# First tails issued by GpSimd, first copy in halves, roots ahead of tables, warming from a constant: the opening of a fused scan and gated-MLP kernel

## Chip, core, metric

The kernel runs on one core of a Trainium2 chip. A core has TensorE (PE in the profile), VectorE (DVE), ScalarE (ACT), GpSimd (POOL), SyncE (SP) and 16 DMA engines that SP, ACT and GpSimd can issue to. The metric is device time in microseconds (us).

## The reference, cut to what matters

```python
xn = layernorm(x)                        # x: 2048 tokens of 448, bf16
Lam_bar = exp(exp(log_dt) * Lam)         # 448 complex states
h[t] = Lam_bar * h[t-1] + B_bar @ xn[t]  # B_bar: 448 x 448 complex
s = 2 * real(h @ C.T) + xn * Dskip
gate, up = xn @ w_gate, xn @ w_up        # 448 -> 1792 each
g = silu((sigmoid(gate) * up) @ w_down)  # 1792 -> 448
out = x + s * g
```

## The kernel before

The 2048 tokens are four chunks (`c`) of 512, and a chunk is four tiles (`j`) of 128 tokens. Products need xn turned, with the 448 features on partitions and tokens along the row: `xnT[c]`, of four blocks of rows (`kt`). A chunk's products are those of the gate and up weights (`g_ps`, `u_ps`, 14 column blocks `ft`), those of B (`bu`), of the down weights (`d_ps`) and of C (`y_ps`). The contraction over 448 is cut into three full blocks of 128 and a tail of 64 rows. The tails of gate and up share a tile: `wt`, gate on partitions 0 to 63 and up on 64 to 127. A gate tail and an up tail then run beside each other in the two halves of the array; L709 issues those of chunk 0. The eight PSUM banks are handed out in turn, so a product that opens a bank waits for the reader of its former content.

The weights come in three parts of column blocks (`w_parts`): part 1 is `gate_1`, `up_1` and `tails_1` (columns 0 to 511). All loads but one of `gate_1` go through SP, and a load is issued only when the one eight places earlier (counting SP's and ACT's) has landed.

The order on each engine is the written order (`keep_order` ties every instruction to the one before it on its engine). Around the change it is this:

- SP issues the loads of x for chunk 0 (tile 0, tile 1, then 2 and 3 together), then part 1 of the weights, `tails_1` last, then part 2, tiles of x of chunk 1, and the transposing loads of B (`bT`).
- TensorE runs 26 products of a zeroed tile `junk` (`warm`), turns the three vectors of the scan (`tp_v`), runs 5 more, turns tile 0 (four turns into `tps[0]`, L289), 2 more, tile 1, 2 more, and then the first gate products on tiles 0 and 1 (`firsts`, L713). Tile 2 and tile 3 are turned between the up products.
- DVE sets constants, takes the moments of tiles 0 and 1 (`ln_stats`: L219, L220), norms both (`ln_norm`, L275), copies the turned tile 0 out of PSUM (`ln_out`, L292), takes the moments of tiles 2 and 3, norms them and copies both.
- ACT takes the root of the variance of a tile in two steps (`ln_inv`, Ln and Exp: L252, L253), tiles 0 and 1, copies the turned tile 1, makes the first rounded angle table (`emit_whole(0)`, L427), takes the roots of tiles 2 and 3, makes the other three tables, loads the table of sine functions and makes sines and cosines (`tables`). Between them come the tanh of chunk 0's first gates (L719).
- GpSimd makes `ident` and a row of indices, and then waits for `dt_b` of ACT (L324), from which it makes `theta`, `turn` (read by `emit_whole`) and `arg_r` (L329 to L331) and the steps of the scan. Later it also relays semaphores: where a sum passes from one half of the array to the other, a `nop` of GpSimd waits for the one product and releases the next (`Sum.add`).

Of the kernel before, what the change touches and what calls it, by code (L numbers as in the profile page):

```python
# [11 lines left out]
BF16 = mybir.dt.bfloat16  # L12
# [7 lines left out]
P = 128  # L20
# [4 lines left out]
KT = 4  # L25
# [47 lines left out]
def kernel(  # L73
# [17 lines left out]
    nc = tc.nc  # L91
    pe, act, dve, pool, sync = nc.tensor, nc.scalar, nc.vector, nc.gpsimd, nc.sync
# [16 lines left out]
    xnT = [w.tile([P, KT, TC], BF16, name=f"xnT{c}") for c in range(3)]  # L109
# [15 lines left out]
    def w_parts(f0, f1):  # L125
        def rows(mat, r0, r1):
            m = mat[r0:r1, f0:f1]
            return m.rearrange("(kt p) f -> p kt f", p=P) if r1 - r0 > P else m

        gate = [(wg[:, 1:3, f0:f1], rows(B_w_gate, 192, 448)), (wg[:, 0, f0:f1], rows(B_w_gate, 0, 128))]  # L130
        up = [(wu[:, 0:2, f0:f1], rows(B_w_up, 0, 256)), (wu[:, 2, f0:f1], rows(B_w_up, 320, 448))]
        tails = [(wt[0:64, f0:f1], rows(B_w_gate, 128, 192)), (wt[64:128, f0:f1], rows(B_w_up, 256, 320))]
        return gate, up, tails

    def load(eng, parts):
        return [eng.dma_start(out=o, in_=i) for o, i in parts]
# [15 lines left out]
    gate_1, up_1, tails_1 = w_parts(0, 512)  # L152
    gate_2, up_2, tails_2 = w_parts(512, 1280)
# [4 lines left out]
    def load_x(c, j0=0, j1=TPC):  # L158
        if c == 3:
            x_t.append(w.tile([P, TPC, D], BF16, name="x3", tag="tc_re"))  # L160
        sync.dma_start(out=x_t[c][:, j0:j1, :], in_=x_src[:, c * TPC + j0:c * TPC + j1, :])
# [15 lines left out]


    junk = w.tile([P, D], BF16, name="junk")
    dve.memset(junk[:, 0:P], 0.0)  # L180
    hpi = w.tile([P, 1], FP32, name="hpi")
    dve.memset(hpi[:], HALF_PI)
    sgn = w.tile([P, 1], FP32, name="sgn")
# [14 lines left out]

    warm_ps = ps.tile([P, P], FP32, name="warm_ps", tag="bank", bufs=8)

    def warm(n, t=ident):
        for _ in range(n):
            pe.matmul(warm_ps[:], lhsT=t[:, 0:P], rhs=t[:, 0:P], start=True, stop=True)  # L203

    def turn_twice(o, src, n):

        for kt in range(3):
            pe.transpose(o[:, kt, 0:n], src[:, kt * P:(kt + 1) * P], ident[0:n, 0:n])
        pe.transpose(o[:, 3, 0:n], src[:, D - P:D], ident[0:n, 0:n])
        pe.transpose(o[0:64, 3, 0:n], src[:, 384:D], ident[0:n, 0:n])  # L210


    mv = w.tile([P, NT, 2], FP32, name="mv")
# [3 lines left out]
    def ln_stats(t):  # L217
        stats = cp.tile([P, 6], FP32, name="stats")
        dve.bn_stats(out=stats[:], in_=x_t[t // TPC][:, t % TPC, :])  # L219
        dve.bn_aggr(out=mv[:, t, :], in_=stats[:])  # L220


    sums = w.tile([P, NT, 2], FP32, name="sums")
# [27 lines left out]
    def ln_inv(t):  # L251
        act.activation(lnv[:, t, :], mv[:, t, 1:2], ACT.Ln, bias=epsb[:])  # L252
        act.activation(rsd[:, t, :], lnv[:, t, :], ACT.Exp, scale=-0.5)  # L253
# [29 lines left out]
    def ln_turn(c, j):  # L283
        xb, cols = xn[c % 3], slice(j * P, (j + 1) * P)
        if c > 0:
            sync.dma_start_transpose(out=xnT[c][:, 0:KT, cols], in_=xb[:, j, :])
            return
        for kt in range(KT):
            pe.transpose(tps[j % 2][:, kt, :], xb[:, j, K_ROWS[kt]:K_ROWS[kt] + P], ident[:])  # L289

    def ln_out(j, by_act=False):
        (act.copy if by_act else dve.tensor_copy)(out=xnT[0][:, :, j * P:(j + 1) * P], in_=tps[j % 2][:])  # L292
# [29 lines left out]
    def emit_dt():  # L322
        vec, dt_b = K["vec"], w.tile([P, KT], BF16, name="dt_b")
        act.activation(dt_b[:], vec[:, :, 0], ACT.Exp)  # L324
        K.update(dt=dt_b, lim=vec[:, :, 1], lre=vec[:, :, 2])
# [99 lines left out]
    def emit_whole(pt):  # L425
        whole = sp.tile([P, HC], I32, name="whole", tag=("ta", "tb", "tcs", "tb")[pt])
        act.activation(whole[:], iota_f[:], ACT.Copy, scale=K["turn"][:, pt:pt + 1])  # L427
        K[pt] = whole
# [480 lines left out]
    def ln_plan(c):  # L909
        own, t0, n = c - 1, c * TPC, 2 if c == 2 else 0  # L910
        for k in range(n):
            at(0, 11 + k, 0.8, lambda t=t0 + k: ln_stats(t))
        t1, m = t0 + n, TPC - n
        steps = [lambda t=t: ln_sum(t) for t in range(t1, t1 + m)] + [lambda: ln_mean(t1, m)]
        steps += [lambda t=t: ln_square(t) for t in range(t1, t1 + m)]
        for k, f in enumerate(steps):
            at(own - 1, (10, 10, 11, 11, 12)[k] if c == 2 else "out%d" % min(k // 2, 3), 0.0, f)
        if n:
            at(0, 12, 0.17, lambda: ln_var(t0, n))
        then = (0, 13) if c == 2 else (own, 1)  # L920
        at(*then, 0.17, lambda: ln_var(t1, m, True))
        at(*then, 0.17, lambda: ln_minus(c))
        at(own, "down0", 0.0, lambda: (ln_pow(t0, TPC), ln_scale(c)))
        for j in range(TPC):
            at(own, "down0", 0.0, lambda j=j: ln_norm(c, j))
        at(own, "down0", 0.0, lambda: [ln_turn(c, j) for j in range(TPC)])

    dummy = w.tile([P, 1], FP32, name="dummy")
    act.add_instruction(mybir.InstLoadActFuncSet(name=nc.get_next_instruction_name(), act_func_set_id=LN_AND_EXP,
                                                 ins=[], outs=[]))  # L930
    warm(26, junk)
    turn_twice(tp_v, rows, 3)
    tps = [ps.tile([P, KT, P], BF16, name="tp_x", tag="bank", bufs=8) for _ in range(2)]
    gus = [(bank("g_ps"), bank("u_ps")) for _ in range(3)]
    warm(5)

    ln_stats(0)
    ln_inv(0)
    emit_vecs()
    ln_stats(1)  # L940
    ln_inv(1)
    emit_dt()
    load(sync, tails_1 + gate_2 + tails_2 + up_2)
    load_x(1, 0, 2)
    emit_angles()
    ln_norm(0, 0)
    ln_turn(0, 0)
    warm(2)
    ln_norm(0, 1)
    ln_turn(0, 1)  # L950
    warm(2)
    ln_out(0)
    ln_out(1, True)
    emit_whole(0)
    for t in (2, 3):
        ln_stats(t)
    for t in (2, 3):
        ln_inv(t)
    for pt in (1, 3, 2):
        emit_whole(pt)  # L960
    act.activation(K["r"][:], K["arg"][:], ACT.Exp)
    act.add_instruction(mybir.InstLoadActFuncSet(name=nc.get_next_instruction_name(), act_func_set_id=SILU_AND_SIN,
# [235 lines left out]
```

## Time and profile before

| | |
|---|---|
| median of 3 runs | 182.26 us (182.23 to 182.44) |
| profiled execution | 182.46 us |
| its span, first to last instruction | 180.7 us |
| mean granted TensorE clock | 0.999 |
| DMA | 14.27 MB, mean 79 GB/s |

Times in the profile are counted from the first instruction of the span. PE's ends are modelled, so TensorE is read by the starts of its products. The bracket behind an instruction gives the idle time of its engine ahead of it and what ended that. SPq lines are DMA issues, which occupy only the queue.

### The profile page before, as it was taken

Reading aid. Unit: us, or ns where it says so; the run is one execution under the profiler, and the core shown is the slowest. Engines: PE = TensorE matmul, PEld = TensorE weight load, DVE = VectorE, ACT = ScalarE, POOL = GpSimd, SP = SyncE. Lnnn points to the kernel's source line nnn. Section 1 sums busy time; section 2 is a strip of 40 time slices with the busy share of each in tenths; the row PEclk is TensorE's granted clock in tenths of the full one; section 3 lists DMA queues with packets and bytes.
Section 4 is the critical chain, followed back from the end, with each engine's and each line's share of the span. In section 5 each row is a group of like instructions: output and inputs, shape, how many; then the busy total and the mean of one; then the engine's idle time right before and its main releaser. Section 6 shows DMA issues by size and latency. Waiting matters only on the chain.

```text
span 180.7 us, 4400 instructions
## 1 busy us (share of the span) xinstructions
PE 176.2 (98%) x1672; PEld 100.2 (55%) x1672; DVE 164.8 (91%) x333; ACT 114.1 (63%) x237; POOL 20.0 (11%) x52
## 2 busy tenths in 40 slices
PE   7999999999999999999999999999999999999992
PEld 7875555555555555555555555555555555545451
DVE  4879999999979999899999999699999989599993
ACT  4799988978099887979177676057048577053100
POOL 3504549321000000001000000000000000000000
PEclk9999999999999999999999999999999999999999
DMA  5998993993335105021610020020001100020011
GB/s 156 305 230 156 281 186 63 307 277 91 72 87 106 33 0 131 5 99 29 75 22 4 0 58 4 0 102 4 0 0 34 29 0 5 0 75 32 0 44 58
DMA packets 26364, 14.27 MB, mean 79 GB/s; under 512 B 16099, under 2 KB 26086, under 8 KB 26342
## 3 DMA queue, kind: packets, MB, share of 16 engines
q1 hardware_dynamic: 26064, 13.72, 31.7%
q8 instruction: 13, 0.21, 0.5%
q10 hardware_dynamic: 278, 0.26, 0.4%
q14 instruction: 9, 0.07, 0.2%
HBM read 7.69 MB, written 1.84 MB: 53 GB/s over the span
## 4 chain that ended last, share of the span: by engine, by line
PE 89%; DVE 9%; issue 1%; DVEq 0%
PE g_ps L517 24%; PE u_ps L517 19%; PE d_ps L517 18%; PE bu L517 12%; PE y_ps L517 10%; PE warm_ps L203 2%; DVE wv L614 1%; DVE o_t L831 1%; PE tp_x L289 1%; DVE hF L749 1%; DVE h L635 1%; DVE o_t L833 1%; DVE t_x L848 1%; PE g_ps L713 1%; PE u_ps L713 1%
## 5 line engine op out<-in xcount | busy, mean ns | idle before, releaser
L517 PE MATMUL u_ps<-xnT,wu 64*128 64x512 bf16 (+1 forms) x336 | 64.3, 370 | 0.0
L517 PE MATMUL g_ps<-xnT,wg 64*128 64x512 bf16 (+1 forms) x336 | 57.3, 370 | 0.0
L752 ACT ACTIVATE sig<-g_ps 128x512 bf16<-128x512 f32 x52 | 29.4, 604 | 27.4 <-PE g_ps L517 26.8
L517 PE MATMUL bu<-xnT,bT 64*128 64x512 bf16 x168 | 37.4, 376 | 0.0
L517 PEld LDWEIGHTS <-wu 64*128 64x128 bf16 x336 | 25.8, 94 | 16.6 <-issue 0.3
L517 PE MATMUL d_ps<-wd,hF 64*128 64x448 bf16 x336 | 32.3, 349 | 0.0
L517 PEld LDWEIGHTS <-wg 64*128 64x128 bf16 x336 | 23.1, 94 | 15.9
L752 ACT CAST ub<-u_ps 128x512 bf16<-128x512 f32 x52 | 29.5, 614 | 0.2
L517 PEld LDWEIGHTS <-hF 64*128 64x128 bf16 x336 | 19.0, 94 | 12.9
L614 DVE TENSOR_TENSOR_SCAN wv<-r_col,st,ta 128x512 bf16<-128x512 f32 x18 | 22.7, 1276 | 0.2
L517 PE MATMUL y_ps<-ct,h 64*128 64x448 bf16 (+2 forms) x203 | 22.3, 343 | 0.1
L749 DVE TENSOR_TENSOR hF<-sig,ub 128x512 bf16<-128x512 bf16 x52 | 21.3, 421 | 0.9 <-ACT ub L752 0.8
L517 PEld LDWEIGHTS <-bT 64*128 64x128 bf16 x168 | 15.8, 94 | 8.4 <-issue 0.2
L517 PE MATMUL g_ps<-xnT,wt 64*128 64x512 bf16 x52 | 19.6, 376 | 0.0
L517 PE MATMUL u_ps<-xnT,wt 64*128 64x512 bf16 x52 | 19.6, 376 | 0.0
L517 PEld LDWEIGHTS <-h 64*128 64x128 bf16 (+1 forms) x203 | 12.8, 95 | 8.9 <-DVE h L635 0.5
L595 ACT CAST bus<-bu 128x512 bf16<-128x512 f32 x24 | 14.5, 606 | 1.3 <-PE bu L517 1.3
L776 ACT ACTIVATE sigd<-d_ps 128x448 bf16<-128x448 f32 x12 | 6.7, 555 | 12.3 <-PE d_ps L517 12.3
L517 PEld LDWEIGHTS <-wt 64*128 64x128 bf16 x104 | 9.8, 94 | 5.3
L1141 PE MATMUL d_ps<-wd,hF 128*128 128x448 bf16 x56 | 10.9, 353 | 0.0
L247 POOL TENSOR_TENSOR rsd<-ve,mhalf 128x2 f32<-128x2 f32 (+1 forms) x4 | 4.9, 1213 | 47.9 <-PE bu L517 39.3
L831 DVE TENSOR_TENSOR o_t<-y_ps,xn 128x448 bf16<-128x448 f32 x12 | 6.9, 617 | 3.5 <-PE y_ps L517 3.5
(152 smaller groups left out, 230.5 us busy)
## 6 DMA issues: line engine op xcount, KB each, us to landing
wd<-in_B_w_down_dram SPq DMA_DIRECT2D x1, 1568.0 KB
out_dram<-o_t SPq DMA_DIRECT2D x6, 224.0 KB, 2.1
x<-in_A_x_dram SPq DMA_DIRECT2D x2, 448.0 KB, 4.2
x<-in_A_x_dram SPq DMA_DIRECT2D x3, 224.0 KB, 3.4
wu<-in_B_w_up_dram SPq DMA_DIRECT2D x2, 256.0 KB
bsw<-bus SPq DMA_DIRECT2D x4, 128.0 KB, 4.5
wsw<-wv SPq DMA_DIRECT2D x8, 64.0 KB, 2.0
c_re<-in_A_C_re_dram SPq DMA_DIRECT2D x1, 392.0 KB, 10.0
```

The lines of the kernel that those rows point to most:

```text
L203: pe.matmul(warm_ps[:], lhsT=t[:, 0:P], rhs=t[:, 0:P], start=True, stop=True)
L247: pool.tensor_tensor(out=rsd[:, t:t + n, :], in0=ve[:, t:t + n, :], in1=mhalf[:, 0:n, :], op=ALU.pow)
L289: pe.transpose(tps[j % 2][:, kt, :], xb[:, j, K_ROWS[kt]:K_ROWS[kt] + P], ident[:])
L517: m = pe.matmul(self.t[:, n0:n1], lhsT=lhsT, rhs=rhs, start=self.done == 1, stop=self.done == self.n)
L595: empty = [lambda cc=cc: act.copy(out=bus[:, cc, :], in_=pst[cc][:]) for cc in range(2)]
L614: dve.tensor_tensor_scan(out=T["wv"][:, cc, :], data0=rb, data1=T["ta"][:, cc, :], initial=(0.0 if c == 0 else st[pt][:, cc, :]), op0=mul, ...
L713: pe.matmul(t[:, n0:n1], lhsT=(wg, wu)[i][:, k, ft * P:(ft + 1) * P], rhs=xnT[c][:, (GATE_K, UP_K)[i][k], n0:n1], start=first, stop=last)
L749: dve.tensor_tensor(out=h[:], in0=sig[:], in1=ub[:], op=ALU.mult)
L752: u.empty = [lambda: act.activation(sig[:], gt[:], ACT.Sigmoid), lambda: act.copy(out=ub[:], in_=ut[:])]
L776: act.activation(sigd[:], ds[j][:], ACT.Sigmoid)
L831: dve.tensor_tensor(out=two_runs(o[:, i, :], HD, HD), in0=two_runs(ys[c, j + 2 * i][:], HD, HD), in1=xn_runs(c, j + 2 * i), op=ALU.add)
L1141: pe.matmul(ds[j][:], lhsT=hF[c, ft][:, j * P:(j + 1) * P], rhs=wd[:, ft, :], start=ft == 0, stop=ft == FT - 1)
```

## The change

1. The two loads of `tails_1` are issued by GpSimd in place of SP, behind a semaphore of the first tile's moments. On GpSimd they stand ahead of `theta`.
2. Tile 0's copy out of PSUM is cut in two: ACT copies blocks 2 and 3, DVE blocks 0 and 1. The turns of tiles 0 to 3 are issued in the order 2, 3, 0, 1.
3. `emit_whole(0)` moves from ahead of the roots of tiles 2 and 3 to behind them.
4. The warming products read a constant of ones that the program sets anyway (one column, read 128 times over) in place of `junk`; DVE's memset of `junk` goes, and the first run of warming products is 28 in place of 26.

```diff
     junk = w.tile([P, D], BF16, name="junk")
-    dve.memset(junk[:, 0:P], 0.0)
...
+    ones = nc.const_aps.tensor(1.0, [P, P], BF16)
...
     def ln_stats(t):
         stats = cp.tile([P, 6], FP32, name="stats")
         dve.bn_stats(out=stats[:], in_=x_t[t // TPC][:, t % TPC, :])
-        dve.bn_aggr(out=mv[:, t, :], in_=stats[:])
+        return dve.bn_aggr(out=mv[:, t, :], in_=stats[:])
...
-        for kt in range(KT):
+        for kt in (2, 3, 0, 1):
             pe.transpose(tps[j % 2][:, kt, :], xb[:, j, K_ROWS[kt]:K_ROWS[kt] + P], ident[:])
...
-    warm(26, junk)
+    warm(28, ones)
...
-    ln_stats(0)
+    moments = ln_stats(0)
+    for tail in load(pool, tails_1):
+        tc.add_manual_dep(tail.ins, moments.ins.name,
+                          mybir.DependencyInfo(mybir.DependencyClass.Sync, mybir.DependencyReason.DATA),
+                          reason="behind the first tiles of x")
     ln_inv(0)
...
-    load(sync, tails_1 + gate_2 + tails_2 + up_2)
+    load(sync, gate_2 + tails_2 + up_2)
...
-    ln_out(0)
+    act.copy(out=xnT[0][:, 2:4, 0:P], in_=tps[0][:, 2:4, :])
+    dve.tensor_copy(out=xnT[0][:, 0:2, 0:P], in_=tps[0][:, 0:2, :])
     ln_out(1, True)
-    emit_whole(0)
     for t in (2, 3):
         ln_stats(t)
     for t in (2, 3):
         ln_inv(t)
-    for pt in (1, 3, 2):
+    for pt in (0, 1, 3, 2):
         emit_whole(pt)
```

## The prediction

> **What bounds the kernel now.** I read the page first, for the engine that is never idle:
>
> ```profile
> PE 176.2 (98%) x1672; PEld 100.2 (55%) x1672; DVE 164.8 (91%) x333; ACT 114.1 (63%) x237; POOL 20.0 (11%) x52
> PE 89%; DVE 9%; issue 1%; DVEq 0%
> ```
>
> The second line is the chain that ended last. TensorE carries it, so what this change does to the time is read from when TensorE gets through the opening. DVE's 9% lie at the end of the span, behind products of TensorE, so they move with it.
>
> Next the timeline of the opening, engine by engine (columns: start, length, instruction, count, and in brackets the idle time before it with what ended it). First how a tile of x is turned and copied:
>
> ```profile
> 0.97 2.96 PE L203 MATMUL warm_ps<-junk 128*128 128x128 bf16 x26 [0.97 <-DVE junk L180]
> 4.70 0.63 PE L289 MATMUL tp_x<-ident,xn 128*128 128x128 bf16 x4
> 5.37 0.43 DVE L292 COPY xnT<-tp_x 128x512 bf16<-128x512 bf16 x1
> 5.40 0.61 PE L289 MATMUL tp_x<-ident,xn 128*128 128x128 bf16 x4
> 5.71 0.62 DVE L219 BATCH_NORM_STATS2 stats<-x 128x6 f32<-128x448 bf16 x1
> 6.05 0.58 ACT L292 COPY xnT<-tp_x 128x512 bf16<-128x512 bf16 x1 [1.03 <-PE tp_x L289]
> 7.49 0.82 DVE L275 TENSOR_SCALAR xn<-x,mv,rsd 128x448 bf16<-128x448 bf16 x2 [0.22 <-ACT rsd L253]
> 7.95 0.40 PE L289 MATMUL tp_x<-ident,xn 128*128 128x128 bf16 x4
> 8.38 0.98 DVE L292 COPY xnT<-tp_x 128x512 bf16<-128x512 bf16 x2
> 8.83 0.28 PE L709 MATMUL g_ps<-xnT,wt 64*128 64x256 bf16 x1
> ```
>
> Three things: tile 1's copy on ACT starts 0.65 behind its first turn (5.40 to 6.05). DVE's copy of tile 0 (5.37) stands directly ahead of the moments of tiles 2 and 3 (5.71), and from those come their norms, turns and copies (7.49, 7.95, 8.38). And four turns keep TensorE 0.43 at 4.70 (the next product starts at 5.13) but 0.23 at 7.95: before about 6.3 it runs at half its later rate.
>
> Then ACT and TensorE up to 20.2, for what is tight behind the opening:
>
> ```profile
> 7.78 1.29 ACT L427 ACTIVATE whole<-iota_f,turn 128x256 int32<-128x256 f32 x3
> 12.30 0.60 ACT L719 ACTIVATE tanh<-g_ps 128x512 f32<-128x512 f32 x1 [0.38 <-PE g_ps L517]
> 16.42 0.30 ACT L353 ACTIVATE cs<-anf,hpi 128x8 f32<-128x8 f32 x1 [0.23 <-DVE anf L347]
> ...
> 19.01 1.08 ACT L752 CAST ub<-u_ps 128x512 bf16<-128x512 f32 x2
> ...
> 19.82 0.38 PE L517 MATMUL u_ps<-xnT,wu 64*128 64x512 bf16 x1
> 20.14 0.37 PE L517 MATMUL bu<-xnT,bT 64*128 64x512 bf16 x1
> ```
>
> The second product of bu starts at 20.14 as the second cast of ub ends (20.09): it needs that bank, and TensorE stands about 0.19 (it would have come at 19.96). ACT's work before it runs without a gap back to 16.42, where it waited for DVE; DVE in turn runs nearly without a gap back to a product at 12.27. So a delay of TensorE at 9.8 goes through DVE (12.27), ACT (16.42) and back to TensorE (20.14) at full size. Behind 20.14 TensorE has no gap that could take it up: its one longer wait, 0.27 at 171.1, is for scans that DVE starts after a product at 156.5. What the opening gains or loses reaches the end.
>
> **The change, part by part.** The sum is made against the profiled execution: 182.46 us, a span of 180.7 and 1.76 around it, 0.20 above the median of 182.26. I carry the difference over to the median.
>
> *Warming from a constant.* The first product no longer waits for the memset (0.80 to 0.91). TensorE can start about as early as DVE did, so at 0.85 (between 0.80 and 0.91) instead of 0.97: 0.12 sooner. Two more products cost 2 x 0.107 (2.67 over 25 steps) = 0.21. Net 0.09 later: tile 0's turns start at 4.79. Their norm ended at 4.64, so nothing hides it.
>
> *First copy in halves.* In the changed program the two halves do not run side by side: ACT's half waits for the last of the four turns, and DVE's half waits for ACT's half (they write one tile). So ACT's half starts 0.65 behind the first turn: 4.79 + 0.65 = 5.44. For its length the nearest row is ACT's copy of 128x256 bf16 at L303, 0.44; the other end is 0.37 (the copy of 512 took 0.58, less 256 elements at ACT's slope from the 12-element cast, 0.17). I take 0.44: DVE's half starts at 5.92, where the whole copy started at 5.37. The moments followed the whole copy by 0.34; behind a half I take 0.25 (ends 0.17 and 0.34). So moments of tile 2 at 6.17, 0.46 late (ends 0.3 and 0.55). What waits behind DVE's half: the moments of tiles 2 and 3, then their norms.
>
> *Roots ahead of tables.* One whole (0.41 from start to start) leaves its place ahead of the roots. Tile 2: moments end at 6.55 + 0.46 = 7.01, both root steps take 0.51 (7.36 to 7.87), root at 7.56, not late for a norm that DVE reaches 0.10 behind the start of the last moments, 7.65 (before: 7.49). Tile 3: moments end 7.27 + 0.46 = 7.73, root 8.28 instead of 7.87, norm at 8.32 instead of 7.91. The move hides part of the delay for tile 2, none for tile 3, which waited for its moments and not for the table.
>
> *Turns and copies of tiles 2 and 3.* Tile 2's copy follows the start of tile 3's norm by 0.47: 8.79. Tile 3's follows it by 0.42: 9.21, ends 9.64 (before 9.36). Its products, 9.41 before, start at 9.69: 0.28 late.
>
> *Tails from GpSimd.* They leave SP (0.56 and 0.58 of issue), so all that SP issues later starts up to 1.2 sooner; no row shows TensorE waiting for any of these loads, so that is worth nothing. On GpSimd the two issues wait for the first moments (3.62) and stand ahead of theta (5.10), turn and arg_r (5.89). No row has a DMA from GpSimd. One issue costs between 0.56 (SP's) and 1.1 (GpSimd's longest, the power at L247); I take 0.9: done at 5.5, theta 0.4 late. Now turn is needed only after the roots, at 8.3, and GpSimd first relays a semaphore between two products at 11.1; both have over 1.5 spare, which also is what an issue of over 1.6 each would use up. Landing: the tails took 3.2 (second) from SP and are needed at 8.83, now about 9.1. GpSimd's second issue starts at 4.6: landing at 7.8 with 3.2, at 9.1 with the 4.5 that the next tails took. I count nothing and keep the upper end as a rival.
> Beside these issues DVE runs the norms of tiles 0 and 1 (4.27, 4.95). The same operation shows what a busy GpSimd does to it:
>
> ```profile
> 21.26 1.12 DVE L275 TENSOR_SCALAR xn<-x,mv,rsd 128x512 bf16<-128x512 bf16 x2
> 27.24 0.73 DVE L275 TENSOR_SCALAR xn<-x,mv,rsd 128x512 bf16<-128x512 bf16 x2
> ```
>
> At 21.26 GpSimd copied cosT and spm; at 27.24 it did 128x4 steps. That is 0.2 a norm. Tile 0's norm would end at 4.84 instead of 4.64: its turns at 4.89, 0.10 behind the 4.79 above. I count 0.10 (ends 0 and 0.4).
> [...]
>
> *ACT behind the roots.* Root of tile 3 0.41 + 0.10 late, then four wholes instead of three: tables and sines 0.94 late, tanh(1) at about 12.77, 0.47 behind 12.30. The 0.23 that ACT waited at 16.42, and DVE's own 0.38, cover it with 0.14 spare. Without that cover it would be added.
>
> Sum: 0.28 + 0.10 = 0.38, rounded to 0.39: **182.65**. Ends: 0.05 (short halves, no disturbance) and 0.8 (long halves, norms held 0.4).
>
> **The rivals.**
> *Not slower: the opening loses its two waits.* TensorE stands 0.11 for tile 2's norm (7.84 to 7.95) and 0.08 for tile 3's copy (9.33 to 9.41). If the halves cost DVE less than the whole copy did (its half starting by 5.45), roots come earlier and both go: 182.07; with the 0.19 at 20.14 gone too, 181.88. It decides at ACT's half ending before 5.45, that is, starting near 5.0. For it: turns at the later rate (0.23 for four) would end so. Against: the rate is the slow one in this stage of the trace. Chance 0.14 of a gain over 0.2%.
> *Norms held by GpSimd.* [...] Chance 0.2.
> *Tails late.* From landing after 9.1 on, each microsecond counts whole. With 1.1 an issue and 4.5 to land: 3.62 + 2.2 + 4.5 = 10.3, 1.2 late: 183.85; half of that 183.25. Against: they leave a queue with a backlog for an empty one. Chance 0.10.
> [...]
> *The change is not felt.* The delay ends up at 0.05 to 0.3, since lags shrink where the rate doubles sooner: 182.3 to 182.55. Chance 0.28, and the first rival's milder end lies in it.
>
> **How the numbers follow.** 0.2% of 182.26 is 0.36 us, about what a measurement of this kernel can tell from no change. My forecast (chance 0.28) stands just outside it, the held norms (0.20) and the late tails (0.10) beyond: slower 0.58; a change not felt is same, 0.28; faster 0.14. The likeliest case's own range is 182.3 to 183.0. For 8 in 10 the range goes to 182.0 below (both waits gone) and 183.4 above (tails half late).
>
> **What would show it.** Right: ACT's half copy at 5.4 to 5.5, DVE's half right behind its end, moments of tile 2 at 6.1 to 6.3, tile 3's norm at 8.3, its tail products near 9.7, bu's second product near 20.5. Wrong: DVE's half by 5.5, turns of tile 2 at 7.85 (the first rival); the products of wt waiting for a DMA (tails); norm of tile 0 beyond 4.9 with a gap ahead of it (GpSimd); a table wait of ACT for turn, or a change of the time outside the span.

## The result and the profile after

The changed kernel takes 183.50 us (median of 5, 183.29 to 183.99), the kernel before 182.34 beside it. The ratio is 1.0066, 95% interval 1.0054 to 1.0079: slower by 1.2 us. The profiled execution took 183.44 with a span of 181.7, 0.98 and 1.0 above those of before.

First TensorE's line and the chain that ended last, from the page of the changed kernel:

```profile
PE 176.7 (97%) x1674; PEld 102.7 (57%) x1674; DVE 164.4 (91%) x332; ACT 114.6 (63%) x238; POOL 21.6 (12%) x54
PE 84%; DVE 9%; DMA 4%; issue 1%; POOL 0%; DVEq 0%
```

A share of DMA, 4%, has come into a chain that held TensorE, DVE and some issue. The timeline of the opening shows where (start, length, instruction, count, and in brackets the idle time before it and what ended that). TensorE:

```profile
0.76 3.15 PE L204 MATMUL warm_ps<-const-bfloat16-1.0 128*128 128x128 bf16 x28 [0.76 <-PEq L1187]
4.68 0.63 PE L290 MATMUL tp_x<-ident,xn 128*128 128x128 bf16 x4
7.86 0.40 PE L290 MATMUL tp_x<-ident,xn 128*128 128x128 bf16 x4
8.58 0.40 PE L290 MATMUL tp_x<-ident,xn 128*128 128x128 bf16 x4
9.62 0.28 PE L710 MATMUL g_ps<-xnT,wt 64*128 64x256 bf16 x1 [0.65 <-DMA wt<-in_B_w_gate_dram]
10.09 0.28 PE L710 MATMUL u_ps<-xnT,wt 64*128 64x256 bf16 x1 [0.18 <-DMA wt<-in_B_w_up_dram]
```

Up to tile 3's turns (8.58, before 8.51) TensorE is 0.07 late. Then it stands for the gate tail and again for the up tail, which in the kernel before were both used at 8.83. The first products behind the tails come 1.1 later, in the kernel before and in the changed one:

```profile
9.79 0.27 PE L517 MATMUL g_ps<-xnT,wg 64*128 64x256 bf16 x1
```

```profile
10.87 0.27 PE L518 MATMUL g_ps<-xnT,wg 64*128 64x256 bf16 x1
```

bu's second product starts at 21.23 in place of 20.14, and the last run of y's products at 177.54 in place of 176.45. The delay of 1.1 at 10 us reaches the end. The clock is no part of it: TensorE's full rate starts at 6.3 in both profiles (four turns take 0.61 at 5.40 and 5.42, and 0.40 at 7.95 and 7.86).

DVE and ACT in the same stretch:

```profile
4.24 0.36 DVE L276 TENSOR_SCALAR xn<-x,mv,rsd 128x448 bf16<-128x448 bf16 x1
5.35 0.37 ACT L957 COPY xnT<-tp_x 128x256 bf16<-128x256 bf16 x1 [0.37 <-PE tp_x L290]
5.75 0.29 DVE L958 COPY xnT<-tp_x 128x256 bf16<-128x256 bf16 x1 [0.40 <-ACT xnT L957]
5.96 0.62 DVE L220 BATCH_NORM_STATS2 stats<-x 128x6 f32<-128x448 bf16 x1
8.12 0.40 DVE L276 TENSOR_SCALAR xn<-x,mv,rsd 128x448 bf16<-128x448 bf16 x1 [0.32 <-ACT rsd L254]
9.01 0.42 DVE L293 COPY xnT<-tp_x 128x512 bf16<-128x512 bf16 x1 [0.16 <-PE tp_x L290]
12.48 0.60 ACT L720 ACTIVATE tanh<-g_ps 128x512 f32<-128x512 f32 x1 [0.58 <-PE g_ps L518]
```

The two halves run one behind the other: DVE's waits 0.40 for ACT's. The moments of tile 2 start 0.25 later than before (5.96 for 5.71), and tile 3's copy ends at 9.43 for 9.36. At 12.48 ACT waits 0.58 for TensorE, so in this trace the roots and tables ahead of it cost nothing.

Last the issues that stand behind the wait, GpSimd's and SP's (SPq lines are issues), and from the DMA part of the page what the tails took from issue to landing (KB each, us):

```profile
3.91 0.81 POOL L136 DMA_DIRECT2D wt<-in_B_w_gate_dram  x1 [1.85 <-DVE mv L221]
4.73 0.53 POOL L136 DMA_DIRECT2D wt<-in_B_w_up_dram  x1
```

```profile
3.62 0.94 SPq L136 DMA_DIRECT2D wg<-in_B_w_gate_dram  x2
```

```profile
wt<-in_B_w_gate_dram POOLq DMA_DIRECT2D x1, 64.0 KB, 5.7
wt<-in_B_w_up_dram POOLq DMA_DIRECT2D x1, 64.0 KB, 5.3
```

The same in the kernel before, the second tail and `gate_2` from SP:

```profile
4.22 0.58 SPq L136 DMA_DIRECT2D wt<-in_B_w_up_dram  x1
4.85 1.10 SPq L136 DMA_DIRECT2D wg<-in_B_w_gate_dram  x2
```

```profile
wt<-in_B_w_up_dram SPq DMA_DIRECT2D x1, 64.0 KB, 3.2
```

GpSimd issues the tails 0.3 and 0.5 later than SP did (3.61 and 4.22), but they need 5.7 and 5.3 to land, at 9.58 and 10.04. SP's issue of the second took 3.2 and landed at 7.45. SP's line `wg` is `gate_2`, two loads of together 576 KB: it is issued at 3.62 in place of 4.85, ahead of both tails.

### The profile page after: what moved, and what is told of

Same layout as the page of the kernel before. It is cut to its first block, busy times and chain, and to the rows that moved or that the text cites. A ratio compares the mean times of both kernels' runs of the same rounds, so it can differ in the third digit from the quotient of the medians.

```text
span 181.7 us, 4405 instructions
## 1 busy us (share of the span) xinstructions
PE 176.7 (97%) x1674; PEld 102.7 (57%) x1674; DVE 164.4 (91%) x332; ACT 114.6 (63%) x238; POOL 21.6 (12%) x54
## 3 DMA queue, kind: packets, MB, share of 16 engines
HBM read 7.69 MB, written 1.84 MB: 52 GB/s over the span
## 4 chain that ended last, share of the span: by engine, by line
PE 84%; DVE 9%; DMA 4%; issue 1%; POOL 0%; DVEq 0%
PE g_ps L518 24%; PE u_ps L518 19%; PE d_ps L518 17%; PE bu L518 12%; PE y_ps L518 10%; DMA wt<-in_B_w_up_dram 3%; DVE wv L615 1%; DVE o_t L832 1%; DMA x<-in_A_x_dram 1%; DVE hF L750 1%; DVE h L636 1%; DVE o_t L834 1%; DVE t_x L849 1%; PE u_ps L710 0%; POOL wt L136 0%
## 5 line engine op out<-in xcount | busy, mean ns | idle before, releaser
L518 PEld LDWEIGHTS <-wu 64*128 64x128 bf16 x336 | 26.3, 94 | 15.6 <-issue 0.3
L518 PEld LDWEIGHTS <-wg 64*128 64x128 bf16 x336 | 23.9, 94 | 15.0
```

The source lines that it names most:

```text
L518: m = pe.matmul(self.t[:, n0:n1], lhsT=lhsT, rhs=rhs, start=self.done == 1, stop=self.done == self.n)
```

## The experiments

The theory after these traces: the whole loss is the landing of the tails, and they land late because `gate_2`, which SP now issues sooner, is on the DMA engines ahead of them. The rivals: the halves and the moved table cost the time and the wait only covers that; or the path from GpSimd itself takes 5.5 us. Each kernel ran beside the kernel before on one chip (its medians there: 182.34 to 182.48).

The table holds what each profile says of the second tail and of TensorE. A median is of all executions of a kernel, the rest of the row of the one that was profiled; kernels that are not in the table are read in the text.

| kernel | gate_2 issued | second tail issued by, at | landed (from issue) | longest wait of TensorE for a tail | median |
|---|---|---|---|---|---|
| before | 4.85 | SP 4.22 | 7.45 (3.2) | none | 182.34 |
| changed | 3.62 | GpSimd 4.73 | 10.04 (5.3) | 0.65 | 183.50 |
| e11, changed again | 3.62 | GpSimd 4.80 | 10.38 (5.6) | 1.33 | 183.80 |
| e1, tails on SP | 4.85 | SP 4.22 | 7.83 (3.6) | none | 182.55 |
| e8, only the tails moved | 3.61 | GpSimd 4.76 | 10.60 (5.8) | 1.32 | 184.02 (one execution) |
| e6, gate_2 nearly as before | 4.63 | GpSimd 4.72 | 9.41 (4.7) | 0.27 | 182.56 |
| e4, gate_2 held longer | 6.89 | GpSimd 4.84 | 7.43 (2.6) | none | 183.04 |
| e9, on SP behind gate_2 | 3.62 | SP 5.29 | 10.29 (5.0) | 1.08 | 183.34 |
| e3, GpSimd at once | 3.62 | GpSimd 2.80 | 7.53 (4.7) | none | 182.51 |
| e7, whole copy | 3.62 | GpSimd 4.71 | 9.72 (5.0) | 0.36 | 183.17 |

**Whose loss it is.** First the tails alone undone:

```diff
-    moments = ln_stats(0)
-    for tail in load(pool, tails_1):
-        tc.add_manual_dep(tail.ins, moments.ins.name, ...)
+    ln_stats(0)
...
-    load(sync, gate_2 + tails_2 + up_2)
+    load(sync, tails_1 + gate_2 + tails_2 + up_2)
```

> The changed kernel with its two first tails issued by SP again, as before, the other three parts kept. Theory (the whole loss is the landing of the tails): they land by 7.5, the tail products start at 9.4 to 9.5, and the time is 182.4 (182.2 to 182.6), since only the last tile's copy, 0.07 later, is left. Rival (the serial halves of the first copy and the moved table cost the time, and the wait for the tails only covers it): 183.0 or more, with TensorE waiting on DVE or ACT between 9 and 21 us.

Measured: 182.55 to 182.41, ratio 1.0007 (0.9986 to 1.0028). The tails land by 7.83 and are used at 8.93 without a wait. With that one part undone the loss is gone, or is below what this measurement can tell.

Then the tails alone done, in the kernel before (e2), and the same kernel measured once more (e8):

```diff
-    ln_stats(0)
+    moments = ln_stats(0)
+    for tail in load(pool, tails_1):
+        tc.add_manual_dep(tail.ins, moments.ins.name, ...)
...
-    load(sync, tails_1 + gate_2 + tails_2 + up_2)
+    load(sync, gate_2 + tails_2 + up_2)
```

> The kernel before, with only the two first tails moved to GpSimd behind the first moments. Theory (landing of the tails): issue near 3.9 and 4.7, landing 9.5 to 10.1, TensorE waits for both, 183.3 (183.0 to 183.6). Rival (halves and table): no more than 182.5.

> [...]

Measured: 183.88 to 182.41, ratio 1.0092 (1.0057 to 1.0126), and 184.02 in the single execution of e8. Moving the tails is enough for the whole loss; it is larger than the 183.3 expected. The first products on tiles 0 and 1 in the two profiles, e2's line first (e8's line numbers lie one higher):

```profile
6.47 2.10 PE L713 MATMUL g_ps<-xnT,wg 128*128 128x128 bf16 x18
```

```profile
6.30 1.18 PE L714 MATMUL g_ps<-xnT,wg 128*128 128x128 bf16 x18 [0.35 <-DVE stats L220]
10.23 0.28 PE L710 MATMUL g_ps<-xnT,wt 64*128 64x256 bf16 x1 [1.32 <-DMA wt<-in_B_w_gate_dram]
```

In e2 TensorE ran at half its later rate (the six up products behind these kept it 1.28 from 8.37, in e8 0.65 from 7.32) until about 10.0 (four turns took 0.56 at 9.65 and 0.39 at 10.38), and the products took 2.10; in e8 they ran at the full rate in 1.18, and TensorE then waited 1.32 for the tails. The two executions take 184.22 and 184.02. So the excess is there without the late clock too. What both share is a later landing (10.63 and 10.60, against 10.04 and 10.38 in the changed kernel). Why it was later with nearly the same issue times (4.85 and 4.76, against 4.73 and 4.80) stays open.

**Why they land late.** Two kernels leave GpSimd's issues where the change put them and only hold SP's loads back:

```diff
-    load(sync, gate_2 + tails_2 + up_2)
-    load_x(1, 0, 2)
...
+    held = ln_stats(2)                  # e6: held = ln_norm(0, 0)
+    for part in load(sync, gate_2 + tails_2 + up_2)[:1]:
+        tc.add_manual_dep(part.ins, held.ins.name, ...)
+    load_x(1, 0, 2)
```

> The changed kernel with SP's loads from gate_2 on held until the moments of tile 2 (issue 6.4 in place of 3.6), so that SP has nothing on the DMA engines when GpSimd's tails pass at 7.3 to 8.9. Theory A (price of the path from GpSimd): the first packet still starts 3.4 behind the issue, at 7.3, and the tails land 9.3 to 10.0: 183.2 to 183.5. Theory B (sharing with SP's transfers): the 32 packets of 0.16 take 0.4 in place of 1.6, landing 8.1 to 8.7, tail products at 9.4 to 9.5, 182.3 to 182.6. By both, B's transposing loads are issued 2.8 later; if TensorE then waits for bT near 20, that part is taken off.

> The changed kernel with SP's loads from gate_2 on held until the norm of tile 0, so that they are issued near 4.85, as in the kernel before, in place of 3.6; GpSimd issues the tails as in the change. Theory (the 1.2 that SP gained let gate_2 onto the engines ahead of the tails): the first packet of the tails starts 1.8 to 2.6 behind the issue in place of 3.4, they land 7.5 to 8.8, and TensorE does not wait: 182.4 to 182.7. Rival (the queue of GpSimd loses to any load in flight): first packet near 7.3, landing 9.2 to 10.0, 183.2 to 183.6.

From the DMA part of e4, then of e6:

```profile
wt<-in_B_w_gate_dram POOLq DMA_DIRECT2D x1, 64.0 KB, 3.0
wt<-in_B_w_up_dram POOLq DMA_DIRECT2D x1, 64.0 KB, 2.6
```

```profile
wt<-in_B_w_gate_dram POOLq DMA_DIRECT2D x1, 64.0 KB, 4.0
wt<-in_B_w_up_dram POOLq DMA_DIRECT2D x1, 64.0 KB, 4.7
```

The same two issues of GpSimd need 5.7 and 5.3 with `gate_2` ahead of them, 4.0 and 4.7 with `gate_2` issued about where the kernel before had it (4.63 for 4.85, between the two), and 3.0 and 2.6 with `gate_2` held back. Even the first packet of the tails moves: 3.39 behind the first issue in the changed kernel, 1.84 in both of these. e4 landed earlier than its own theory said (7.05 and 7.43 for 8.1 to 8.7), since that had left the first packet at 7.3. e6's second tail, at 9.41, landed later than its theory's 7.5 to 8.8: it was issued 0.1 behind `gate_2`. The path from GpSimd is not what takes 5.5 us; what is on the engines ahead of it is. The packets of the tails pass in the same stretch as those of SP's loads: between 7.0 and 9.2 of the changed kernel 0.13 MB in GpSimd's queue (q0) beside 0.57 MB in q1, 317 GB/s together. The three pairs above agree with a sharing of the engines. Why the first packet waits no run here shows.

Their times are less simple. e4 has no wait for a tail, and yet 183.04, ratio 1.0028 (1.0006 to 1.0049). Its products of `up_2` give the place:

```profile
13.85 0.38 PE L518 MATMUL g_ps<-xnT,wt 64*128 64x512 bf16 x1
14.34 0.89 PE L518 MATMUL u_ps<-xnT,wu 64*128 64x512 bf16 x6
```

In the kernel before the second followed the first by 0.02 (13.70, 13.72), here by 0.49: the larger load of `up_2`, issued at 9.07, landed at 14.29. The hold moved the wait to the next weights. e6 comes out at 182.56, ratio 1.0015 (1.0002 to 1.0029), and in its profiled execution (182.84, 0.28 over the median) TensorE still waits a little:

```profile
9.45 0.28 PE L710 MATMUL u_ps<-xnT,wt 64*128 64x256 bf16 x1 [0.27 <-DMA wt<-in_B_w_up_dram]
```

The control takes GpSimd out and leaves the place behind `gate_2`:

```diff
-    moments = ln_stats(0)
-    for tail in load(pool, tails_1):
-        tc.add_manual_dep(tail.ins, moments.ins.name, ...)
+    ln_stats(0)
...
-    load(sync, gate_2 + tails_2 + up_2)
+    load(sync, gate_2 + tails_1 + tails_2 + up_2)
```

> The changed kernel with the two tails on SP, but behind gate_2 instead of ahead of it: they are issued at about 4.6 and 5.2, at nearly the times of GpSimd's issues (3.9 and 4.7), and nothing comes from GpSimd. Theory (what counts is how much of gate_2 is on the DMA engines ahead of the tails, not which queue brings them): landing 9.6 to 10.7, 183.3 to 184.2, as in the changed kernel or worse. Rival (the queue of GpSimd is what is slow): landing 7.9 to 8.7, no wait, 182.4 to 182.7.

```profile
10.10 0.28 PE L710 MATMUL g_ps<-xnT,wt 64*128 64x256 bf16 x1 [1.08 <-DMA wt<-in_B_w_gate_dram]
```

```profile
wt<-in_B_w_up_dram SPq DMA_DIRECT2D x1, 64.0 KB, 5.0
```

Measured: 183.34 to 182.48, ratio 1.0051 (1.0030 to 1.0072). SP's own transfers land as late as GpSimd's once `gate_2` is ahead of them. With e4, where GpSimd's land in 3.0 and 2.6, the rival that blames the queue of GpSimd falls.

Then the tails from GpSimd ahead of `gate_2`, without the wait for the moments:

```diff
-    moments = ln_stats(0)
-    for tail in load(pool, tails_1):
-        tc.add_manual_dep(tail.ins, moments.ins.name, ...)
+    ln_stats(0)
+    load(pool, tails_1)
```

> The changed kernel with the wait for the first moments left out: GpSimd issues the tails as soon as its index row is done, near 2.1 and 2.9. Theory A (a transfer issued by GpSimd takes its 5.3 to 5.7 from issue to landing wherever it stands): landing 7.4 to 8.6, before the 9.1 to 9.4 at which they are needed, 182.2 to 182.6. Theory B (most of that time is what SP's transfers take from it on the shared DMA engines): the engines are fuller at 5 to 7 us (350 to 400 KB a us) than at 7 to 9, so landing 8.0 to 9.5 and the loads of gate_1 and up_1 land later too, 182.3 to 183.0. Rival (GpSimd's transfers do not start before 7.3, whatever the issue): 183.4.

Measured: 182.51 to 182.41, ratio 0.9997 (0.9981 to 1.0014). Issued at 2.02 and 2.80, the tails land at 6.42 and 7.53, 4.4 and 4.7 behind, and nothing waits for them. The first landed earlier than either theory said, the second within A's 7.4 to 8.6, and with less time behind its issue than in the changed kernel (4.7 for 5.3), which A alone does not give. The change's loss is gone with its wait: it was the place behind the first moments, with `gate_2` let go ahead of them, that cost 1.1.

**The other parts.** The copy made whole again, once with the tails on GpSimd (e7) and once with the tails on SP as in e1 (e5):

```diff
-    act.copy(out=xnT[0][:, 2:4, 0:P], in_=tps[0][:, 2:4, :])
-    dve.tensor_copy(out=xnT[0][:, 0:2, 0:P], in_=tps[0][:, 0:2, :])
+    ln_out(0)
```

> The changed kernel with tile 0's copy whole on DVE, the tails still on GpSimd. Theory (landing alone sets the time, the copy is hidden behind it): tails land 9.5 to 10.1, the time is that of the changed kernel, 183.3 to 183.6. Rival (the halves add to the wait): 183.0 to 183.2.

> The changed kernel with the tails on SP and tile 0's copy whole on DVE again: what is left of the change is the roots ahead of tables and the warming from a constant. Theory (the halves delay DVE, the two other parts are free): the moments of tile 2 start at 5.7 in place of 5.96, its norm at 7.2 to 7.3, TensorE no longer waits for it nor for tile 3's copy, and the time is up to 0.2 below the kernel before, 182.2 to 182.4, and 0.1 to 0.3 below the run with halves and tails on SP (182.55). Rival (two more warming products or the moved table cost as much as the halves): 182.5 or more.

And the changed kernel itself once more:

> The changed kernel itself once more, for the spread of the tails' landing and beside the others on one chip. By all theories 183.3 to 183.9, tails landing 9.4 to 10.2; the part of the time over 182.5 should be TensorE's wait for them in this profile, within 0.15.

e7 measured 183.17 to 182.38, ratio 1.0050 (1.0036 to 1.0065); e11 183.80 to 182.48, ratio 1.0073 (1.0056 to 1.0089). By the numbers expected, e7 went to the rival, but its tails also landed at 9.72, 0.3 to 0.7 before those of the changed kernel's two profiles, and TensorE still waited 0.36 for them. With the landing this spread, e7 does not say what the halves cost. In e11 TensorE waits 1.33 for the tails, and its profiled execution is 1.30 over 182.5: within the 0.15 given; its landing at 10.38 is later than the 9.4 to 10.2 expected.

e5 measured 182.40 to 182.38, ratio 1.0011 (0.9992 to 1.0029). Its moments of tile 2 start at 5.59 and its tails are used at 8.54, 0.29 sooner than before. Its profiled execution (182.68) does not keep that:

```profile
14.54 0.39 PE L518 MATMUL u_ps<-xnT,wu 64*128 64x512 bf16 x2 [0.32 <-DMA wu<-in_B_w_up_dram]
```

Its twelve times fall into two groups, six from 182.19 to 182.28 and six from 182.53 up. The profile is of the second group, so that the wait is in the other six too is not shown. Against e1 (182.55) the whole copy is worth 0.15 by the medians; the intervals of the two overlap, so the price of the halves is seen in the trace (0.25 on DVE) and not in the time.

**Does a version beat both?** Two candidates follow. The first joins e3 and e5 (tails from GpSimd at once, whole copy). The second is e5 with `up_2` ahead of `tails_2`:

```diff
-    load(sync, tails_1 + gate_2 + tails_2 + up_2)
+    load(sync, tails_1 + gate_2 + up_2 + tails_2)
```

> The version that the runs point to: tails from GpSimd without the wait for the moments, tile 0's copy whole on DVE, roots ahead of tables, warming from a constant. Theory: tails land 6.4 to 7.6, TensorE waits neither for them nor for tile 2's norm, and SP's loads of up_2, issued 1.2 sooner, no longer land at 14.5 as they did with the tails on SP: 182.1 to 182.3, below the kernel before. Rival (three queues at once delay the tiles of x or gate_1, or the gain of 0.2 in the opening does not reach the end): 182.4 or more.

> The run with the whole copy and the tails on SP, with one thing changed: SP issues up_2 ahead of tails_2. In that run TensorE had gained 0.27 by 9.5 and lost it at 14.54, waiting for the second load of up_2, and its times fell into two groups (182.2 and 182.55). Theory (up_2, last of SP's weights ahead of B's transposing loads, sometimes lands late): with up_2 earlier nothing waits near 14, and the time is 182.1 to 182.3 in nearly all runs. Rival (the last load in that place is late whatever it is, or the two groups come from the time at which the full clock starts): TensorE waits for tails_2 near 13.4, or the times fall into the same two groups, median 182.4 or more.

e10 measured 182.53 to 182.48, ratio 1.0014 (0.9997 to 1.0030): no gain. In its profiled execution the tails go first, and `up_1` is late in their place:

```profile
8.17 0.83 PE L714 MATMUL u_ps<-xnT,wu 128*128 128x256 bf16 x6 [0.81 <-DMA wu<-in_B_w_up_dram]
```

That execution took 183.22, 0.7 over the median, so the wait is not what the median pays; why the median gains nothing stays open.

e12 measured 182.41 to 182.34, ratio 0.9994 (0.9969 to 1.0019). Its profiled execution, 182.24, kept 0.22 from the opening to the end and waits nowhere near 14. But its 12 times run from 182.24 to 182.85: not the two groups of e5, and with a median at the 182.4 that the rival named, not the 182.1 to 182.3 of the theory. No version is faster than the kernel before by more than can be measured.

## Why the prediction was wrong

Forecast 182.65 (182.0 to 183.4), measured 183.50. (The two terms of its sum make 0.38, not the 0.39 that was used; that changes nothing.) The sign was right by luck: the terms that were to make the kernel slower, the halves and the held norms, came to 0.07 in the trace, and the loss came from a term counted as nothing. The mechanism stood among the rivals as "Tails late", with a chance of 0.10; its price, each microsecond of landing after 9.1 whole, was right: landing at 10.04, TensorE 1.07 and 1.18 late at tile 3's first gate and up tail products, the span 1.0 longer. Its way there was another: it reached 10.3 by slow issues (second done at 5.8) and 4.5 to land, and the runs show a second issue at 4.73 and 5.3 to land.

**The step that failed** is the landing in the part on the tails: "I count nothing and keep the upper end as a rival". Behind it lay two statements.
- "They leave a queue with a backlog for an empty one". The queue was empty (its 64 packets are all of the tails), the DMA engines were not: from 3.55 to 5.9 they moved 336 GB/s. e9 shows that behind `gate_2` SP's own queue lands the tails at 10.29, e4 that without `gate_2` GpSimd's lands them at 7.43.
- "all that SP issues later starts up to 1.2 sooner; no row shows TensorE waiting for any of these loads, so that is worth nothing". In these runs what started sooner delayed what started later: with `gate_2` at 3.62 the second tail took 5.3, with it at 6.89 (e4) 2.6. The sum asked who waits for `gate_2`, and not whom `gate_2` makes wait. With `gate_2` nearly back at its old time (e6, 4.63) the time is 182.56.

The upper end, 4.5 from issue to landing, was the time of `tails_2` in the kernel before, which also stands behind `gate_2`; that was the nearer row. With it and the issue at 4.73 the landing is 9.2, just past the 9.1 at which the tails were needed, so that row alone would have cost about 0.1; the other 0.8 of the landing is in no row of before, and why the tails took 5.3 and not 4.5 is not shown. In e4, where SP issued `gate_2` only at 6.89, the two tails took 3.0 and 2.6; behind `gate_2` the second took 5.0 to 5.8 in five profiles.

**Warming**: TensorE starts at 0.76, not 0.85, so the two added products are covered, and tile 0's turns start at 4.68 (predicted 4.79). **Halves**: serial as predicted, ACT's at 5.35 (5.44) and 0.37 long (0.44, other end 0.37), the moments of tile 2 0.25 late (0.46). Up to the tails the opening stands at 0.07 in the trace, near the prediction's lower end of 0.05, and e1 measures 0.14 with an interval that holds zero. **Roots**: tile 3's norm at 8.12 (8.32). ACT waits for TensorE at 12.48, but there the late tails cover it. e1 tests the cover: its second tanh no longer waits, ACT still waits 0.23 for DVE at 16.53, and bu's second product comes 0.11 late, as much as the tail products, so nothing is added. **GpSimd's issues**: 0.81 and 0.53 (0.9 each). **Norms held by GpSimd** did not happen: tile 0's norm took 0.36 beside the first issue, 0.37 before, and tile 1's 0.43 beside the second, 0.40 before. The 0.10 counted for it was nothing, and the rival at 0.20 fell. No run shows the 0.4 that the upper end of the sum gives to held norms: the norm of tile 0 started at 4.24, inside the issue from 3.91 to 4.72, and ended at 4.60. **From 20.14 to the end** the delay passes at full size, as said.

## What to carry to other kernels

When a load is taken out of a queue, look first at what moves up in its place: here `gate_2` moved up from 4.85 to 3.62, and the second of the moved tails took 5.3 to land in place of 3.2. Take the landing time of a moved load from the row of a transfer that stands behind the same bytes, not from the row of the load itself, and leave room above it: here the row said 4.5, and five profiles 5.0 to 5.8. What protected the early load here was its place ahead of the large one, in both queues: ahead of `gate_2` the second tail landed at 7.83 from SP (e1) and at 7.53 from GpSimd (e3), behind it at 10.29 (e9) and 10.04 (the changed kernel).

## What the runs showed of the hardware

- The start of the full rate of TensorE differs from execution to execution of nearly the same opening. The five warming products at 4.15 to 4.20 took 0.71 or 0.72 in eight profiles (before, changed, e1, e2, e4, e6, e9, e10), 0.63 in e11, 0.52 in e5 and 0.45 to 0.47 in e3, e7 and e8. Four turns took 0.61 at 5.44 in e1, 0.40 at 5.48 in e11, and still 0.56 at 9.65 in e2. What sets the start no run shows. For this kernel it means that two traces of the opening can be compared only with an eye on it: e5's lead of 0.28 at 9.5 may come partly from an earlier full rate (four turns took 0.40 at 4.69, in the kernel before 0.63 at 4.70).
- The first packet of GpSimd's tails started 3.3 to 3.5 behind the issue in the five profiles in which SP had issued `gate_2` 0.3 to 0.4 earlier, and 1.84 behind it in e6 and e4, in which SP issued it later. Where GpSimd issued at 2.02, with `gate_1` and `up_1` close by (e3, e10), it was 2.76 and 2.94. The same landing of one kernel differed by 0.34 between two profiles (10.04 and 10.38).
